# A GpSimd copy puts the first transposing load of x behind the first gate rows, one core, geglu FFN

## The chip, the cores and the metric

One core of a Trainium2 chip runs the whole kernel in one launch. The metric is the device time of that launch in microseconds (us); the time before is 273.48 us, the median of three runs (273.24, 273.48, 274.23). A difference of less than about 0.5% (1.37 us) can't be told from no change here.

## The reference

```python
B, S, D, F = 32, 32, 1024, 3584           # all inputs bf16
def reference(x, w_gate, w_up, w_down):
    return (_gelu(x @ w_gate) * (x @ w_up)) @ w_down   # tanh gelu
```

x is flattened to 1024 tokens by 1024 features. Random normal inputs, scaled by 0.05.

## The kernel before, in words

Both products are done by a Strassen-like scheme with seven half-size products (names with 11, 12, 21, 22 are the quadrants). Everything is written in an order of its own by hand (`tc.manual_schedule()`), so each engine's instructions stand in the order of the program text, and semaphores are put in where a tile is written and then read or written again. Semaphores of loads are taken in turn from eight slots, so a load also waits for the one eight loads before it.

Tokens are the columns (halves of `NB` = 512), features the rows (`DT` = 8 blocks of 128). `b11`, `b12`, `b21`, `b22` are the four quadrants of x with features on partitions; the first index is the feature half. `b21` is features 512 to 1023 of tokens 0 to 511: four blocks k = 0..3. Blocks 0 and 1 come by an ordinary load into `x_nat` and are transposed on TensorE in `transposed(dt)` (through `tp`, copied by VectorE into `b21`). Blocks 2 and 3 come by one transposing transfer, `load_xT(0, KD + KQ, DT)`. In the profile all four quadrants are named `b`.

The first work of TensorE is a set of products "ahead": gate columns in groups of `KB` = 4 blocks of 128, feature half 2 only, against `b21`. Group i has its weights in `a12_ahead[i]` (profile: `a12a` for i = 0, 1, `a12b` for i = 2 to 5), loaded by `load_ahead(i, k0, k1)`, where k0 to k1 are the feature blocks. `product_ahead(ps, i, j, k0, k1)` makes the matmuls; in the profile they are L288. The order on TensorE at the start is:

- `NWARM` = 6 matmuls on constants, to fill the time until `x_nat` lands (L258),
- `transposed(0)` (L266), then `NFILL` = 4 short 128-column matmuls on constants (L273),
- group 0, block k = 0, tokens 0 to 255 (four columns j), then `transposed(1)`, then the rest of k = 0 and 1 of group 0, in halves of 256 tokens,
- group 1, k = 0 and 1: eight matmuls of 512 columns,
- then, for each of the four columns of group 0, k = 2 and k = 3 in turn; then the same for group 1; then groups 2, 3, 4 and 5 with chunk 0's first product in between.

From there chunk follows chunk (`for ci in range(NCH)`, two column blocks of 128 each, seven products by `prod`, L277), with sums s1 to s4 of weights on GpSimd (L171 to L174) and t1 to t4 of x on VectorE (`tt`, L349 to L360). A second part multiplies by w_down (L429).

Loads stand on SyncE's queue (SP, L212 for `load_ahead`, L219 for transposing ones, L136 for the weight chunks) but for the probe, the second half of `x_nat` and k = 0, 1 of group 1, which are issued by ScalarE. SyncE's order around the change is: `x_nat` block 0; group 0 k = 0; group 0 k = 1; the transposing transfer of `b21` blocks 2, 3; group 0 k = 2, 3; group 1 k = 2, 3; groups 2 and 3 by halves; `wu` and `wg` of chunk 0; group 4; then `b11` and `b12` by transposing transfers, group 5, `b22`. GpSimd, after it has made `ident`, has nothing to do until `wu` has landed.

Of the kernel before, what the change touches and what calls it, by code (L numbers as in the profile page):

```python
# [13 lines left out]
def kernel(  # L14
# [20 lines left out]
    nc = tc.nc  # L35
# [14 lines left out]
    KD = DT // 2  # L50
# [4 lines left out]
    KQ = DT // 4  # L55
    HF = FT // 2
    MT = NB // P
    NWARM = 6
    NFILL = 4
    KB = 4  # L60
    QF = HF // 2
    batches = [(0, KB), (KB, QF), (QF, QF + KB), (QF + KB, HF)]
# [50 lines left out]
    a12_ahead = [ring.tile([P, KD, KB * P], bf16, name="a12a", tag="ring") for _ in range(2)]  # L113
    b11 = xpool.tile([P, KD, NB], bf16, name="b11")
    b21 = xpool.tile([P, KD, NB], bf16, name="b21")
# [81 lines left out]
    with tc.manual_schedule():  # L197
        def load_nat(eng, dt, p0, p1):
            eng.dma_start(  # L199
                out=x_nat[:, p0:p1, dt * P : (dt + 1) * P],  # L200
                in_=xf[p0 * P : p1 * P, (KD + dt) * P : (KD + dt + 1) * P].rearrange("(b p) d -> p b d", p=P),
            )
# [7 lines left out]
        def load_ahead(i, k0, k1, eng=nc.sync, j0=0, j1=KB):  # L210
            f0 = i * KB
            eng.dma_start(  # L212
                out=a12_ahead[i][:, k0:k1, j0 * P : j1 * P],
                in_=wg_r[:, KD + k0 : KD + k1, (f0 + j0) * P : (f0 + j1) * P],
            )

        def load_xT(nb, d0, d1):
            t = ((b11, b12), (b21, b22))[d0 // KD][nb]
            nc.sync.dma_start_transpose(  # L219
                out=t[:, d0 % KD : (d1 - 1) % KD + 1, :], in_=xf[nb * NB : (nb + 1) * NB, d0 * P : d1 * P]  # L220
            )

        load_ahead(0, 0, 1)
        load_nat(nc.scalar, 1, 0, NB_P)
        load_ahead(0, 1, 2)
        load_xT(0, KD + KQ, DT)
        load_ahead(1, 0, KQ, nc.scalar)
        a12_ahead += [spool.tile([P, KD, KB * P], bf16, name="a12b", tag=t) for t in ("s2", "s4", "s1", "s3")]
        for i in (0, 1):
            load_ahead(i, KQ, KD)  # L230
        def load_halves(i):
            for k in range(0, KD, KQ):
                load_ahead(i, k, k + KQ)
# [28 lines left out]
        def transposed(dt):  # L262
            for half, tp in enumerate(tps[dt]):
                p0 = half * HALF
                for b in range(HALF):
                    nc.tensor.transpose(  # L266
                        tp[:, b * P : (b + 1) * P], x_nat[:, p0 + b, dt * P : (dt + 1) * P], ident
                    )
                nc.vector.tensor_copy(b21[:, dt, p0 * P : (p0 + HALF) * P], tp)

        transposed(0)
        for _ in range(NFILL):
            nc.tensor.matmul(warm_ps[:, :P], lhsT=ones_w, rhs=ones_w, start=True, stop=True)  # L273
# [351 lines left out]
```

## Time and profile before

| | |
|---|---|
| median of three runs | 273.48 us |
| the profiled execution | 273.29 us |
| its span (first to last instruction) | 271.5 us |
| PE (TensorE) busy | 267.4 us (98%) |
| DVE (VectorE) / ACT (ScalarE) / POOL (GpSimd) busy | 202.8 / 115.6 / 120.2 us |
| moved by DMA | 35.86 MB, mean 132 GB/s |
| DMA share, 0 to 12 us | 7 to 9 tenths and more, in slices of 6.8 us |

Times inside the span are counted from its start; some 1.8 us of the execution lie around the span. A timeline row gives the start, how long the row lasted, the engine, the line and operation, out<-in, and how many instructions were merged; the bracket tells how long the engine sat idle before it and what ended that. A row of DMA issues gives out<-in, the issuing queue, the count, the size of one, and the median us from issue to landing. A queue's "DMA" row (SPq) is only the issue; the landing is later.

### The profile page before, as it was taken

How to read it: one execution, taken by the hardware profiler on the slowest of the kernel's cores; microseconds unless marked ns; L12 is line 12 of the kernel's file. 1: busy time of each engine (PE TensorE's matmuls, PEld its weight loads, DVE VectorE, ACT ScalarE, POOL GpSimd, SP SyncE). 2: the span in 40 equal slices, each digit the busy share in tenths (PEclk: the TensorE clock that was granted, in tenths of full speed). 3: DMA queues.
4: the chain of work that ended last, by engine and by line, in shares of the span. 5: the costliest groups of instructions: out<-in, count | busy, mean ns of one | idle time of the engine just before them, and what ended most of it. 6: DMA issues, size and time to landing. Idle time of an engine off the chain costs nothing.

```text
span 271.5 us, 3422 instructions
## 1 busy us (share of the span) xinstructions
PE 267.4 (98%) x1216; PEld 192.9 (71%) x1216; DVE 202.8 (75%) x205; ACT 115.6 (43%) x189; POOL 120.2 (44%) x60
## 2 busy tenths in 40 slices
PE   8999999999999999999999999999999999999995
PEld 4444776886787788688688687764458888888883
DVE  1448998886876876876776478469999999998621
ACT  2435766445544643745636635434000307870000
POOL 1090099977995994994994996000000000000000
DMA  7999230514505505505224290006981537865211
GB/s 173 325 245 251 52 104 21 150 38 117 157 1 153 156 2 155 139 15 157 81 76 127 49 325 4 0 2 202 356 253 60 158 112 260 273 196 163 73 42 58
DMA packets 56672, 35.86 MB, mean 132 GB/s; under 512 B 9936, under 2 KB 56656, under 8 KB 56656
## 3 DMA queue, kind: packets, MB, share of 16 engines
q1 hardware_dynamic: 53264, 33.17, 43.2%
q10 hardware_dynamic: 3392, 2.49, 2.8%
q8 instruction: 9, 0.15, 0.2%
q14 instruction: 7, 0.06, 0.1%
HBM read 31.72 MB, written 2.10 MB: 125 GB/s over the span
## 4 chain that ended last, share of the span: by engine, by line
PE 97%; DMA 1%; SPq 0%; DVE 0%; issue 0%
PE psA L277 38%; PE psA L429 24%; PE psC L277 19%; PE psC L429 7%; PE psA L288 5%; PE psC L288 3%; DMA a12a<-in_w_gate_dram 1%; PE psC L593 1%; SPq L199 0%; DVE o_last L594 0%; PE tp L266 0%
## 5 line engine op out<-in xcount | busy, mean ns | idle before, releaser
L277 PE MATMUL psA<-t,s 128*128 128x512 f32 x224 | 57.2, 397 | 0.0
L250 ACT ACTIVATE h<-c 128x512 bf16<-128x512 f32 x56 | 34.6, 629 | 41.6 <-DVE c L307 41.6
L277 PEld LDWEIGHTS psA<-t,s 128*128 128x128 f32 x224 | 42.1, 188 | 9.5
L171 POOL TENSOR_TENSOR s<-wu 128x1024 fp32r<-128x1024 bf16 x13 | 29.5, 2270 | 30.6 <-DMA wu<-in_w_up_dram 19.7
L172 POOL TENSOR_TENSOR s<-s,wg 128x1024 fp32r<-128x1024 f32 x14 | 32.0, 2284 | 15.0 <-DVE s L171 13.9
L277 PE MATMUL psA<-b,wg 128*128 128x512 bf16 x128 | 29.4, 380 | 0.0
L174 POOL TENSOR_TENSOR s<-wg,wu 128x1024 fp32r<-128x1024 bf16 x13 | 28.4, 2182 | 0.0
L277 PE MATMUL psA<-t,a22r 128*128 128x512 f32 x112 | 27.9, 391 | 0.0
L277 PE MATMUL psC<-t,s 128*128 128x512 f32 x112 | 27.9, 391 | 0.0
L277 PE MATMUL psC<-b22r,s 128*128 128x512 f32 x112 | 27.7, 389 | 0.0
L307 DVE TENSOR_TENSOR c<-sn,psA 128x512 f32<-128x512 f32 x32 | 21.8, 683 | 6.7 <-PE psA L277 5.9
L312 ACT COPY sn<-psC 128x512 f32<-128x512 f32 x28 | 16.3, 588 | 21.9 <-PE psC L277 14.9
L277 PEld LDWEIGHTS psC<-t,s 128*128 128x128 f32 x112 | 21.0, 188 | 4.5
L277 PEld LDWEIGHTS psA<-t,a22r 128*128 128x128 f32 x112 | 21.0, 188 | 4.5
L277 PEld LDWEIGHTS psC<-b22r,s 128*128 128x128 f32 x112 | 21.0, 188 | 4.4
L307 DVE TENSOR_TENSOR c<-sn,psC 128x512 f32<-128x512 f32 x28 | 19.2, 688 | 6.4 <-PE psC L277 6.4
L277 PEld LDWEIGHTS <-wg 128*128 128x128 bf16 x128 | 11.8, 98 | 15.3 <-issue 2.4
L406 DVE TENSOR_TENSOR lo<-c,h 128x512 bf16<-128x512 f32 x14 | 21.3, 1522 | 0.9
L173 POOL TENSOR_TENSOR s<-wg,s 128x1024 fp32r<-128x1024 bf16 x10 | 21.6, 2159 | 0.8
L312 ACT COPY sn<-psA 128x512 f32<-128x512 f32 x32 | 18.3, 592 | 5.5 <-PE psA L277 5.4
L307 DVE TENSOR_TENSOR c<-ahead,psA 128x512 f32<-128x512 f32 x24 | 16.4, 688 | 4.0 <-PE psA L277 2.4
L325 DVE TENSOR_TENSOR hi<-h,psA 128x512 bf16<-128x512 bf16 x14 | 9.6, 687 | 11.5 <-PE psA L277 11.5
(87 smaller groups left out, 381.1 us busy)
## 6 DMA issues: line engine op xcount, KB each, us to landing
wu<-in_w_up_dram SPq DMA_DIRECT2D x14, 512.0 KB, 4.0
wdb<-in_w_down_dram SPq DMA_DIRECT2D x12, 512.0 KB, 4.4
wg<-in_w_gate_dram SPq DMA_DIRECT2D x9, 512.0 KB, 5.1
wdb<-in_w_down_dram SPq DMA_DIRECT2D x12, 384.0 KB, 4.4
v<-in_w_down_dram SPq DMA_DIRECT2D x4, 512.0 KB, 6.2
out_dram<-o_sb ACTq DMA_DIRECT2D x15, 128.0 KB, 1.7
a12b<-in_w_gate_dram SPq DMA_DIRECT2D x6, 256.0 KB, 4.8
wg<-in_w_gate_dram SPq DMA_DIRECT2D x6, 256.0 KB, 4.7
```

The costliest lines, as they stand in the source:

```text
L171: yield engs[0].tensor_tensor(s1, a21, a22, ADD)
L172: yield engs[1].tensor_tensor(s2, s1, a11, SUB)
L173: yield engs[2].tensor_tensor(s4, a12, s2, SUB)
L174: yield engs[3].tensor_tensor(s3, a11, a21, SUB)
L250: nc.scalar.activation(h, src, ACT.Gelu_apprx_tanh)
L277: nc.tensor.matmul(ps, lhsT=lhs[:, k, :], rhs=rhs[:, k, :], start=(start and k == 0), stop=(k == KD - 1), skip_group_check=True,)
L288: nc.tensor.matmul(ps[:, cols], lhsT=a12_ahead[i][:, k, j * P : (j + 1) * P], rhs=b21[:, k, cols], start=(k == 0 and not cols.start), stop ...
L307: tt(t, s, ps, ADD)
L312: nc.scalar.copy(t, ps)
L325: tt(g_of(ft)[:, :NB], h0, psa, MUL)
L406: tt(g_of(ft)[:, NB:], added(sn5[fl], psa[fl]), h1[fl], MUL)
L429: nc.tensor.matmul(banks[m], lhsT=lhs(k)[:, m * P : (m + 1) * P], rhs=rhs(k), start=(start and k == 0), stop=(k == HF - 1), skip_group_che ...
```

## The change

Four things are edited. Group 0's k = 2 is loaded by a transfer of its own, which stands ahead of the transposing transfer, and k = 3 follows behind it. GpSimd copies one element of group 0's k = 0 into `b21`, where the transposing transfer will write; so the copy waits for that load, and the transposing transfer waits for the copy. The loads of group 1 (k = 2, 3) keep their order. Three short matmuls on constants are made in place of four.

```diff
-    NFILL = 4
+    NFILL = 3
...
         load_ahead(0, 0, 1)
         load_nat(nc.scalar, 1, 0, NB_P)
         load_ahead(0, 1, 2)
+        load_ahead(0, KQ, KQ + 1)
+        nc.gpsimd.tensor_copy(b21[:1, KQ, :1], a12_ahead[0][:1, 0, :1])
         load_xT(0, KD + KQ, DT)
         load_ahead(1, 0, KQ, nc.scalar)
         a12_ahead += [spool.tile([P, KD, KB * P], bf16, name="a12b", tag=t) for t in ("s2", "s4", "s1", "s3")]
-        for i in (0, 1):
-            load_ahead(i, KQ, KD)
+        load_ahead(0, KQ + 1, KD)
+        load_ahead(1, KQ, KD)
```

`KQ` is 2, `KD` is 4, `DT` is 8. SyncE has one instruction more, GpSimd one, TensorE one matmul and one weight load less; otherwise the order on every engine is as before.

## The prediction

> **What bounds the kernel now.** I read the chain that ended last first, by engine on the page, then its pieces of the first 14 us.
>
> ```profile
> PE 97%; DMA 1%; SPq 0%; DVE 0%; issue 0%
> ```
>
> ```profile
> 1.24 3.41 DMA a12a<-in_w_gate_dram
> 4.65 0.05 issue
> 4.70 0.39 PE psC L288 x2
> ```
>
> TensorE is the bound, and the only DMA on its chain is the load of group 0's k = 0 (issued at 1.24, landed at 4.65). TensorE's timeline shows the hole that it leaves and where the transferred blocks are first used:
>
> ```profile
> 3.71 0.49 PE L273 MATMUL psA<-const-bfloat16-1.0 128*128 128x128 bf16 x4
> 4.70 0.39 PE L288 MATMUL psC<-b,a12a 128*128 128x256 bf16 x2 [0.50 <-DMA a12a<-in_w_gate_dram]
> ...
> 8.44 1.03 PE L288 MATMUL psC<-b,a12a 128*128 128x512 bf16 x4
> 9.30 2.75 PE L288 MATMUL psA<-b,a12a 128*128 128x512 bf16 x12
> ```
>
> 0.50 us of idle end at 4.70; after that no row has a gap. The row at 8.44 is group 0 with k = 2 and 3: k = 2 and block 2 of `b21` are needed at 8.44, and k = 3 one matmul later, (9.30 - 8.44) / 4 = 0.22 on, at 8.66. Now SyncE's queue, and the landings of the issues at 2.25, 3.63, 15.66 and 19.68 (the DMA view of short windows around each):
>
> ```profile
> 1.24 0.96 SPq L212 DMA_DIRECT2D a12a<-in_w_gate_dram  x2
> 2.25 1.34 SPq L219 DMA_TRANSPOSE b<-in_x_dram  x1
> 3.63 1.08 SPq L212 DMA_DIRECT2D a12a<-in_w_gate_dram  x2
> 4.76 2.01 SPq L212 DMA_DIRECT2D a12b<-in_w_gate_dram  x4
> ```
>
> ```profile
> b<-in_x_dram SPq DMA_TRANSPOSE x1, 4.9
> a12a<-in_w_gate_dram SPq DMA_DIRECT2D x1, 256.0 KB, 4.3
> b<-in_x_dram SPq DMA_TRANSPOSE x1, 5.0
> b<-in_x_dram SPq DMA_TRANSPOSE x1, 5.3
> ```
>
> The transposing transfer lands at 2.25 + 4.9 = 7.15, so it has 1.3 us in hand; k = 2, 3 land at 3.63 + 4.3 = 7.93 and have 0.5 us. Those two small reserves are what the change spends.
>
> **The change part by part.**
>
> *The wait.* The transposing transfer can go out only when k = 0 has landed, GpSimd has copied, and SyncE has seen it. GpSimd's start after a landing: `wu`, issued at 6.81, landed 6.8 us later at 13.6, and its sum began at 13.74: 0.14. The copy itself isn't in the trace; the smallest GpSimd rows are 0.10 us (memsets of 128x1) and 0.29 (the select of `ident`). I take 0.15, as it is nearest to the smallest, and 0.06 for SyncE to go on (the gap between its issues is 0.05). That is 0.35 us after the landing, bounds 0.25 to 0.5: at 4.65 + 0.35 = 5.0 in place of 2.25. On GpSimd only the sum of 13.74 is queued behind the copy, so that costs nothing there. On SyncE every later load is queued behind it.
>
> *The transposing transfer itself.* Its price isn't one number: 4.9 us for this one of two blocks, 5.0 and 5.3 for the later ones of four blocks. The latter have 256 KB more, 0.9 us at the some 290 GB/s at which the DMA view of 16 to 17 us moves them, so 4.1 and 4.4 for two blocks. Bounds 4.1 to 4.9; I take 4.4, the row at 19.68, since it had only two loads in front of it, as here (k = 1 and k = 2 are the last ones before). It lands at 5.0 + 4.4 = 9.4.
>
> *k = 3.* It is issued when SyncE is through with the transposing issue (1.34 us), and goes through the same queue. Before, 256 KB landed 7.93 - 7.15 = 0.78 after the transposing transfer; 128 KB makes 0.39. So k = 3 lands at 9.4 + 0.39 = 9.8. It was needed at 8.66: TensorE ends its wait 1.1 us later than that matmul ran before. Block 2 alone (9.4 against 8.44) would cost 0.96; k = 3 comes last and decides. With the bounds of the price the shift is 0.8 to 1.6.
>
> *k = 2 ahead.* Issued at about 2.25 in the place of the transposing transfer, 128 KB, landed about as fast as its neighbour k = 1 (3.7 us, so near 6.0): long before 8.44. It takes nothing off the path, because its partner k = 3 is late. Without this edit k = 2 and 3 would land 0.39 later still.
>
> *What the freed start gives.* If k = 0 lands sooner, the 0.50 us of idle before 4.70 shrinks. But a TensorE that starts sooner only waits longer at k = 3; an earlier landing counts by letting the copy and the transfer go sooner. Does it land sooner? In the DMA view of 2.25 to 4.2 us the engines move some 200 GB/s, less than the 350 after 6.5 us, so there is something in the way. But the transposing packets are 256 B like those of `x_nat`, and the transfer was issued at 2.25, 1.01 us after k = 0. I take the landing unchanged, with 4.1 as the other bound (x_nat's 2.4 us after issue would give 3.64; TensorE has `b21` only by 4.0, when the first copy of the 0.51 us row at 3.74 is over).
>
> The Trainium skill, "DMA: Bandwidth & Descriptors", section "Rules for kernel authors", says that a transpose next to ordinary DMAs needs nothing, and that a DMA should be issued early and waited for late; by that the wait only spends reserve. No row here separates the two, since every transposing issue has others about it.
>
> *The fill.* One matmul of 128 columns less: (0.49 - 0.21) / 3 is about 0.1 us at most, hidden in the 0.50 of idle. If that cover is gone (k = 0 at 4.1) it is worth under 0.1 us, which the wait at k = 3 takes again.
>
> *What is queued behind on SyncE.* Group 1's k = 2, 3 had been issued at about 4.25; now SyncE reaches it at 5.0 + 1.34 + 0.55 + 0.1 = 7.0, 2.75 later. Landings move less, because the queue was full of data before: the transposing transfer is 9.4 - 7.15 = 2.25 later, less the 0.39 of k = 2 that went ahead, so about 1.9. Group 1's second half then lands at 8.7 + 1.9 = 10.6, needed at 10.16 + 1.1 = 11.3; group 2 at 9.4 + 1.9 = 11.3, needed at 11.89 + 1.1 = 13.0. The narrowest place behind is on VectorE:
>
> ```profile
> 20.80 2.29 DVE L349 TENSOR_TENSOR t<-b,b 128x2048 fp32r<-128x2048 bf16 x1 [1.10 <-DMA b<-in_x_dram]
> 25.13 2.29 DVE L355 TENSOR_TENSOR t<-b,t 128x2048 fp32r<-128x2048 bf16 x1 [0.26 <-DMA b<-in_x_dram]
> ...
> 39.10 0.68 DVE L307 TENSOR_TENSOR c<-sn,psA 128x512 f32<-128x512 f32 x1
> ```
>
> t1 and t2 wait for `b12` and `b22`, the last loads of this queue, and VectorE then works without a break until 41.7. Its add at 39.10 ends at 39.78 and must be over before TensorE goes on in that bank, in the second half of its row at 40.13 (L277, psA<-t,a22r, eight matmuls in 1.81), at 41.03: 1.25 us in hand. VectorE slides by 1.9, TensorE by 1.1: the reserve falls to 0.45 and holds.
>
> **The sum.** 273.29 + 1.1 = 274.4 against the profiled execution's own time (span 272.6). The median of the runs is 0.19 above it, which would make 274.6; I give 274.5.
>
> **The rivals.**
>
> *The first rows come sooner.* The transposing issue is what holds them up, and k = 0 lands at 4.1. For it: the low rate from 2.3 to 4. Against: its packets stand behind those of k = 0. The copy chain gives 4.45, the transfer 8.85, k = 3 9.25: 0.6 late, 273.29 + 0.6 = 273.9. (Bounds 0.3 to 1.1.)
>
> *A transposing transfer on a quiet queue is as quick as a plain one.* `x_nat` took 2.4 us for 128 KB; 0.4 more for the other half makes 2.8. It lands at 7.8, and k = 3, issued at 6.4, at 6.4 + 2.4 = 8.8, 0.14 late: 273.4. With the first rows at 4.1 as well, nothing is late, the 0.50 of idle is gone and the time is 272.8. Against: no transposing row is under 4.1 when brought to two blocks, and the issue alone takes 1.34. The Trainium skill, "DMA: Bandwidth & Descriptors", section "Anatomy of one DMA — SWDGE (gpsimd) path", has a fixed 2.0 us and 436 GB/s, for another issuing path; an estimate by it is 2.6 us for 256 KB, against the row's 4.9, so the trace disagrees.
>
> *Slower: the queue slides whole.* The later loads slide by SyncE's 2.75 us and not by 1.9. Then t1, t2 and the add of 39.10 slide by 2.75, over the 1.25 in hand, and TensorE is 1.5 late whatever it lost at k = 3: 274.8, 275.0 from the median, 0.55% up. It decides from a slide of 1.25 + 1.1 = 2.35 on. For it: the queue is served in order. Against: DMA is full from 6 us on, and a full queue slides by the hole in its data.
>
> *The clock falls in the wait.* The 128x512 matmuls of L258 show a mean of 623 ns against 379 later: TensorE starts at half rate. If a wait of over 1 us sent it back, up to 1.7 us more, 276. Against: the 0.50 us hole at 4.2 left the matmuls after it at full rate.
>
> **How the numbers follow.** The forecast (first rows unchanged, 0.8 to 1.6 late) 52%; first rows sooner 18%; transfer as quick as a plain one 7%, and with a gain 3%; the queue slides whole 14%; the clock 3%; 3% for a gain of over 0.5% that no row shows (all idle before 8.44 would have to go). Slower by over 0.5% (1.37 us; less can't be told from no change): the upper third of the forecast, 16%, with 14% and 3%: 33%. Faster 3%, the rest, 64%, within. The range leaves out the gains below and the clock above: 273.2 to 275.6; the forecast's own is 274.1 to 275.1.
>
> **What would show it.** Transposing issue on SyncE at about 5.0 and a GpSimd copy just before; L288 idle before k = 2 or 3, at 8.4 to 8.7, for about 1.1 us, released by a12a (or by `b`); none at 20 to 42. Wrong if that idle is absent or over 1.7, if the first L288 row starts before 4.4, or if TensorE has a gap behind VectorE near 41.

## The result, and the profile after

The changed kernel takes 274.83 us (median of 17 runs, 273.93 to 275.83), the kernel before 273.68 beside it (17 runs): ratio 1.0041, 95% interval 1.0027 to 1.0054, so 1.15 us slower, 0.7 to 1.5. With 17 runs of each this can be told from no change, though it lies under the 1.37 us named at the top. The profiled execution took 275.7 us, its span is 273.9, 2.4 more than before; 1.5 of that lies behind VectorE's last instruction, where only the last store is left (4.06 us in place of 2.54). Of the other profiles below one alone has such a tail (3.8 us, the kernel with the longer wait); a second profile of the changed kernel has 2.57. So the tail isn't counted to the change.

The chain by engine on the page, which was PE 97% and DMA 1% before:

```profile
PE 95%; issue 2%; DVE 2%; DVEq 0%
```

A load is no longer on it; VectorE is. SyncE's waits up to 10 us (who waited for whom: total, times, longest), GpSimd's timeline from 1 to 6 us and SyncE's timeline show the wait that was put in:

```profile
SPq L219 <- POOL b L227: 1.5, 1, 1.5
```

```profile
4.02 0.18 POOL L227 COPY b<-a12a 1x1 bf16<-1x1 bf16 x1 [2.71 <-DMA a12a<-in_w_gate_dram]
```

```profile
1.24 1.43 SPq L212 DMA_DIRECT2D a12a<-in_w_gate_dram  x3
4.22 1.34 SPq L219 DMA_TRANSPOSE b<-in_x_dram  x1
5.61 1.04 SPq L212 DMA_DIRECT2D a12a<-in_w_gate_dram  x2
6.70 2.00 SPq L212 DMA_DIRECT2D a12b<-in_w_gate_dram  x4
```

k = 0 landed at 3.96 (2.7 us after its issue, 3.4 before), the copy ran, and the transposing transfer went out at 4.22 in place of 2.25. What stands behind it on SyncE's queue goes out 1.9 to 2.0 us later (5.61 against 3.63, 6.70 against 4.76). The landings of the issues at 4.22 and at 5.61 (short windows of the DMA view):

```profile
b<-in_x_dram SPq DMA_TRANSPOSE x1, 3.3
a12a<-in_w_gate_dram SPq DMA_DIRECT2D x1, 128.0 KB, 3.1
```

The transposing transfer, 4.9 us before, takes 3.3, and is there at 7.53, only 0.4 later than before; k = 3 is there at 8.70. TensorE's timeline:

```profile
4.11 0.59 PE L290 MATMUL psC<-b,a12a 128*128 128x256 bf16 x2
5.77 0.61 PE L290 MATMUL psA<-b,a12a 128*128 128x256 bf16 x2
6.44 0.38 PE L290 MATMUL psA<-b,a12a 128*128 128x256 bf16 x2
8.82 1.03 PE L290 MATMUL psC<-b,a12a 128*128 128x512 bf16 x4
```

It starts on the gate rows at 4.11 in place of 4.70, but at half rate until 6.2 (0.6 us for two matmuls, then 0.38), and reaches k = 2 at 8.82, where k = 2, k = 3 and the transferred blocks are in: no gap there, 0.38 late. The gap is at 42 us. VectorE's timeline, TensorE's (before first, then after), and after's chain of work that ended last around it:

```profile
27.03 2.29 DVE L357 TENSOR_TENSOR t<-b,t 128x2048 fp32r<-128x2048 bf16 x1 [1.08 <-DMA b<-in_x_dram]
...
41.01 0.68 DVE L309 TENSOR_TENSOR c<-sn,psA 128x512 f32<-128x512 f32 x1
```

```profile
40.13 1.98 PE L277 MATMUL psA<-t,a22r 128*128 128x512 f32 x8
41.94 1.98 PE L277 MATMUL psC<-b22r,s 128*128 128x512 f32 x8
```

```profile
40.61 2.35 PE L279 MATMUL psA<-t,a22r 128*128 128x512 f32 x8
42.79 2.01 PE L279 MATMUL psC<-b22r,s 128*128 128x512 f32 x8
```

```profile
41.01 0.69 DVE c L309
...
41.74 1.21 PE psA L279 x4
```

t2 (VectorE's second sum of x) waits for `b22` until 27.03 (25.13 before), the add of 39.10 stands at 41.01, and TensorE goes on behind it at 41.74. TensorE was 0.48 late at 40.61 and is 0.85 late at 42.79. Its last product starts 0.88 later than before (before first, then after):

```profile
265.40 3.23 PE L593 MATMUL psC<-wdb,a_last 128*128 128x384 bf16 x28
```

```profile
266.28 3.23 PE L595 MATMUL psC<-wdb,a_last 128*128 128x384 bf16 x28
```

So between 43 and 266 us nothing more is lost.

### The profile page after: what moved, and what is told of

It is laid out like the page before. It is cut to its first block, busy times and chain, and to the rows that moved or that the text cites. A ratio compares the mean times of both kernels' runs of the same rounds, so it can differ in the third digit from the quotient of the medians.

```text
span 273.9 us, 3411 instructions
## 1 busy us (share of the span) xinstructions
PE 267.9 (98%) x1202; PEld 193.3 (71%) x1215; DVE 202.2 (74%) x205; ACT 115.6 (42%) x189; POOL 120.7 (44%) x61
## 4 chain that ended last, share of the span: by engine, by line
PE 95%; issue 2%; DVE 2%; DVEq 0%
PE psA L279 36%; PE psA L431 24%; PE psC L279 18%; PE psC L431 7%; PE psA L290 5%; PE psC L290 3%; DVE c L309 1%; PE psC L595 1%; PE psA L260 1%; PE tp L268 0%; DVE s L171 0%; PE psA L275 0%; DVE o_last L596 0%; DVE lo L408 0%; DVEq L309 0%
## 5 line engine op out<-in xcount | busy, mean ns | idle before, releaser
L174 POOL TENSOR_TENSOR s<-wg,wu 128x1024 fp32r<-128x1024 bf16 x13 | 29.4, 2261 | 0.0
L279 PE MATMUL psA<-b,wg 128*128 128x512 bf16 x119 | 27.8, 379 | 0.6
```

What stands on the lines that cost most here:

```text
L174: yield engs[3].tensor_tensor(s3, a11, a21, SUB)
L279: nc.tensor.matmul(ps, lhsT=lhs[:, k, :], rhs=rhs[:, k, :], start=(start and k == 0), stop=(k == KD - 1), skip_group_check=True,)
```

## The experiments

Three theories were set against each other. The queue theory: the wait makes SyncE's later loads late, `b22` last, and VectorE passes it on. The clock theory: TensorE's longer half rate at the start is the loss. The start theory: the wait lets the first gate rows land sooner. "After" below is the changed kernel; ratios are to the kernel before.

**The order without the wait.**

```diff
-        nc.gpsimd.tensor_copy(b21[:1, KQ, :1], a12_ahead[0][:1, 0, :1])
```

> The changed kernel without the copy: k = 2 goes ahead of the transposing transfer, three short matmuls, no wait. Queue theory (the time is lost because every load behind the wait comes about 1.9 us later, and VectorE's add near 41 us is late): the transposing issue is back near 2.7, b22 lands near 25, no gap near 42, 273.7 us as before (ratio 1.000, at most 0.001 off). Clock theory (TensorE's half rate lasts longer, to 6 us in place of 3.9, since a fill is missing): half rate to 6 us again, 0.4 to 1.1 us slower than before. Start theory (only the wait lets the first gate rows land early): k = 0 lands at 4.5 to 4.7 as before, not at 4.0.

273.55 us, ratio 0.9997 (0.9980 to 1.0015): no change. VectorE's timeline has t2 back:

```profile
24.86 2.29 DVE L356 TENSOR_TENSOR t<-b,t 128x2048 fp32r<-128x2048 bf16 x1 [0.15 <-DMA b<-in_x_dram]
```

So k = 2 as a transfer of its own and the missing fill cost nothing that can be told, though the half rate lasted to 4.9. k = 0 landed at 4.23, sooner than the 4.5 to 4.7 which the start theory asked for.

**The wait alone.**

```diff
         load_ahead(0, 1, 2)
+        nc.gpsimd.tensor_copy(b21[:1, KQ, :1], a12_ahead[0][:1, 0, :1])
         load_xT(0, KD + KQ, DT)
```

> The kernel before with the copy alone: k = 2 and 3 in one transfer behind the transposing one, four short matmuls. Queue theory: as slow as the changed kernel or up to 0.4 us slower, 274.6 to 275.2, with a gap near 42 us. Clock theory, if the fourth fill is what counts: full rate from 3.9 us, and 273.7 or less. Start theory: the first row of L288 starts near 4.1.

274.47 us, ratio 1.0034 (1.0015 to 1.0053): the loss belongs to the wait. It is 0.1 us under the expected 274.6; the gap near 42 is there, with 0.24 us. Here TensorE waits for k = 2 and 3 as well, where the prediction had put the loss; its timeline:

```profile
9.25 1.04 PE L289 MATMUL psC<-b,a12a 128*128 128x512 bf16 x4 [0.87 <-DMA a12a<-in_w_gate_dram]
```

The half rate lasted to 4.9 with four fills, as with three above.

**A longer wait.**

```diff
-        nc.gpsimd.tensor_copy(b21[:1, KQ, :1], a12_ahead[0][:1, 0, :1])
+        nc.gpsimd.tensor_copy(b21[:1, KQ, :1], a12_ahead[0][:1, 1, :1])
```

> The changed kernel with the copy reading k = 1 (landed at 5.16) in place of k = 0 (3.96): the wait is 1.2 us longer. Queue theory: b12 and b22 land 1.2 us later than in the changed kernel, VectorE's chain slides 1.2 more, the time is 1.2 us more, about 276.0, with a gap of about 1.5 us near 42 us or an equal one before it near 9 us. Clock theory: no change against the changed kernel, 274.8.

276.05 us (six runs), ratio 1.0084 (1.0064 to 1.0105): 1.2 us more than after, as the queue theory gives, and against the clock theory (full rate from 3.4 here, the soonest of all). SyncE's waits, and t2 on VectorE's timeline:

```profile
SPq L219 <- POOL b L227: 3.4, 1, 3.4
```

```profile
28.51 2.29 DVE L357 TENSOR_TENSOR t<-b,t 128x2048 fp32r<-128x2048 bf16 x1 [0.62 <-DMA b<-in_x_dram]
```

Up to 3 us this kernel does the same as after, and yet k = 0 landed at 5.04 and not at 3.96. So in this profile SyncE's wait is 1.9 us longer than in after's and not 1.2, and the last product 1.43 later: the way is as expected, and that the medians differ by just 1.2 is in part chance. TensorE waits in both places, 1.0 us for block 2 and k = 3 at 9 to 10 us and some 0.4 near 43.

**Less work on VectorE.**

```diff
-        chunk0 = sums(0, *[nc.gpsimd] * 3, nc.vector)
+        chunk0 = sums(0, *[nc.gpsimd] * 4)
```

> The changed kernel with chunk 0's sum s3 on GpSimd (idle from 20 to 34 us) and not on VectorE: VectorE's chain is 1.22 us shorter ahead of the add near 41 us. Queue theory: the gap near 42 us is gone, and only what TensorE is late at 8.8 us is left: 0.4 to 0.5 us less than the changed kernel, 274.3. Clock theory: the gap at 42 isn't what counts, so 274.8 as the changed kernel.

274.72 us, ratio 1.0042 (1.0020 to 1.0064): no better than after, so not what the queue theory expected. The timelines of GpSimd and VectorE say why this was no clean test:

```profile
22.61 2.12 POOL L174 TENSOR_TENSOR s<-wg,wu 128x1024 fp32r<-128x1024 bf16 x1
```

```profile
22.99 3.88 DVE L351 TENSOR_TENSOR t<-b,b 128x2048 fp32r<-128x2048 bf16 x1 [2.87 <-DMA b<-in_x_dram]
28.00 2.28 DVE L357 TENSOR_TENSOR t<-b,t 128x2048 fp32r<-128x2048 bf16 x1
```

GpSimd's sum came to lie beside t1 (VectorE's first sum of x), which took 3.88 us in place of 2.29; the 1.22 us taken off VectorE came back as 1.59, and TensorE waited 0.53 us for t2 itself.

**The adds first.** The same question without moving work:

```diff
                 prod(psa[fl], s3[fl], t3, False)
-                tt(g_of(ft)[:, NB:], added(sn5[fl], psa[fl]), h1[fl], MUL)
+                sn5[fl] = added(sn5[fl], psa[fl])
+            for fl, ft in enumerate(fts):
+                tt(g_of(ft)[:, NB:], sn5[fl], h1[fl], MUL)
```

> The changed kernel, with VectorE's two adds that read TensorE's bank (c<-sn,psA) made one after the other and the two long multiplications behind them, in every chunk: the add that TensorE waits for near 42 us comes 2 us earlier, GpSimd's work stays as it is. Queue theory, with VectorE as the last step: the gap near 42 us is gone, and of the 0.88 us that the changed kernel's last product is late only the lateness at 12 us is left (0.0 to 0.8, by how late k = 3 is): 274.2 to 274.6, 0.3 to 0.5 us less than the changed kernel. If k = 3 alone sets the end: no change against the changed kernel, 274.8.

274.36 us, ratio 1.0032 (1.0014 to 1.0051). On VectorE's timeline the second add is now 1.0 us behind the first and not 2.7, and TensorE's has no gap near 42:

```profile
37.98 0.69 DVE L309 TENSOR_TENSOR c<-sn,psA 128x512 f32<-128x512 f32 x1
39.02 0.69 DVE L309 TENSOR_TENSOR c<-sn,psA 128x512 f32<-128x512 f32 x1 [0.35 <-ACT h L252]
```

```profile
40.39 1.98 PE L279 MATMUL psA<-t,a22r 128*128 128x512 f32 x8
42.21 1.98 PE L279 MATMUL psC<-b22r,s 128*128 128x512 f32 x8
```

The last product is 0.26 late; 0.23 of it is there at 12.12 already (11.89 before), behind a wait for k = 3. In time that is 0.5 us less than after by the medians and 0.2 by the ratios, and the intervals overlap; that the add is the last step is shown by the profile, not by the time.

**The control: the same adds in the kernel before.**

> The kernel before with the same two adds first: the control. The add there has 1.25 us in hand, so both theories expect no change: 273.7, ratio 1.000, at most 0.001 off.

273.32 us, ratio 0.9991 (0.9977 to 1.0004): no change that can be told. Set beside this, the wait still costs 1.04 us (0.4%) with the adds first, nearly the 1.15 that it costs without, while the two profiles differ by 0.50 (265.66 and 265.16 in the table below). So the add isn't the only place with little in hand, and no run shows in time that moving it wins anything back; what is late in the executions that were not profiled is open.

**The transposing transfer later in the queue, with the wait.**

```diff
-        load_xT(0, KD + KQ, DT)
         load_ahead(1, 0, KQ, nc.scalar)
...
         load_ahead(0, KQ + 1, KD)
         load_ahead(1, KQ, KD)
+        load_xT(0, KD + KQ, DT)
```

> The changed kernel with the transposing transfer, its wait included, behind k = 3 and group 1's second half on SyncE's queue: the wait of SyncE falls to some 0.3 us, because it gets there at 3.9 when k = 0 has about landed. Queue theory (it is the idle SyncE that costs): b22 lands at 25 to 25.6, no gap near 42, block 2 of b21 lands near 8.2: 273.4 to 273.9, the time of before. If it is the later transposing issue that costs and not what stands behind it: 274.6 to 274.8.

273.94 us, ratio 1.0017 (1.0001 to 1.0033): less than half of the loss by the middle values, though the interval overlaps with that of after. SyncE's timeline and VectorE's:

```profile
1.24 2.38 SPq L212 DMA_DIRECT2D a12a<-in_w_gate_dram  x5
4.67 1.34 SPq L219 DMA_TRANSPOSE b<-in_x_dram  x1
```

```profile
26.35 2.29 DVE L357 TENSOR_TENSOR t<-b,t 128x2048 fp32r<-128x2048 bf16 x1 [0.99 <-DMA b<-in_x_dram]
```

Two loads have moved out of the idle time. It was still 1.0 us long, not 0.3, since k = 0 landed at 4.41; `b22` came later than expected for the same reason, and the last product is 0.15 late. The transposing issue itself is later than in after (4.67 against 4.22) and the time is less: by the middle values, what stands behind it counts.

**The late place without the wait.**

> The same late place of the transposing transfer, without the copy, so without a wait. Queue theory: 273.4 to 273.9, equal to the one with the wait within 0.2 us. Start theory (the wait lets the first gate rows land early): L288 starts at 4.2 to 4.7 here and at 4.1 with the wait; if landings of k = 0 scatter by themselves, there is no such order.

273.63 us, ratio 1.0002 (0.9985 to 1.0020): as before. The transposing issue is at 3.67 and SyncE is never idle. The first row on gate rows starts at 4.28, sooner than the 4.46 with the wait, against the start theory.

**The order without the wait, with the adds first.**

> What the experiments point to: no wait, k = 2 on its own ahead of the transposing transfer, the two adds first. Queue theory: b22 lands near 24.7, TensorE without a gap from 4.3 on, 273.2 to 273.5, at most 0.2% under the kernel before and 1.2 us under the changed kernel. A theory in which the adds alone make up for the wait gives no more than the 0.4 us that they gave there.

273.67 us, ratio 1.0007 (0.9985 to 1.0028): not a version that beats the kernel before. TensorE waits for no load behind 4.52 us in it, but the half rate lasted to 5.7, and the last product is 0.41 late by that alone.

**The changed kernel, a second profile.**

> The changed kernel once more, for a second profile of it. Queue theory: gap near 42 us again, TensorE's last product (L595) 0.8 to 1.3 us later than the 265.40 of before, whenever the clock goes up. Clock theory: if the clock goes up near 4 to 5 us, as in four of the other profiles, the last product is at most 0.5 us late.

276.07 us in its one run, above the slowest of after's 17. TensorE was at full rate by 4.66, where its gate rows start, and the last product 2.57 late: against the clock theory, and twice what the queue theory had expected. k = 0 landed at 4.62 and SyncE stood until 4.88; `b22` came 3.6 us late. Now several reserves are used up, in TensorE's timeline and VectorE's:

```profile
25.32 1.90 PE L290 MATMUL psC<-b,a12b 128*128 128x512 bf16 x8 [0.62 <-DMA a12b<-in_w_gate_dram]
...
31.20 2.09 PE L279 MATMUL psA<-t,s 128*128 128x512 f32 x8 [0.41 <-DVE t L357]
```

```profile
28.77 2.29 DVE L357 TENSOR_TENSOR t<-b,t 128x2048 fp32r<-128x2048 bf16 x1 [1.50 <-DMA b<-in_x_dram]
...
42.75 0.67 DVE L309 TENSOR_TENSOR c<-sn,psA 128x512 f32<-128x512 f32 x1
```

**All profiles together.** The start of t2 on VectorE beside the start of TensorE's last product. t2 waits for `b22`, but in three profiles VectorE was busy until it started: late without the wait, order with the adds first, and the one with less work on VectorE.

| kernel | t2 starts | last product starts | between |
|---|---|---|---|
| before | 25.13 | 265.40 | 240.27 |
| order without the wait | 24.86 | 265.26 | 240.40 |
| late, without the wait | 24.85 | 265.32 | 240.47 |
| late, with the wait | 26.35 | 265.55 | 239.20 |
| after | 27.03 | 266.28 | 239.25 |
| the wait alone | 27.23 | 266.44 | 239.21 |
| wait for k = 1 | 28.51 | 267.71 | 239.20 |
| after, second profile | 28.77 | 267.97 | 239.20 |
| before, adds first | 24.82 | 265.16 | 240.34 |
| order, adds first | 25.18 | 265.81 | 240.63 |
| after, adds first | 26.68 | 265.66 | 238.98 |
| after, less on VectorE | 28.00 | 266.64 | 238.64 |

In all five profiles with the wait and VectorE's work unchanged, the last product follows t2 at 239.20 to 239.25 us, whatever TensorE did up to then. In the profiles without the wait there is 1.07 us or more in hand. With the wait and VectorE's work changed (the last two rows) the 239.2 is undercut: it was VectorE's chain from t2 to the add.

## Why the prediction came out

The forecast was 1.1 us on the profiled execution; by the medians it is 1.15. The number held, and the place was another: the one that the third rival named, not k = 3. All three signs that the prediction gave for being wrong are in the profile of after: no idle time at 8.4 to 8.7, gate rows from 4.11 on, and a gap behind VectorE at 42. So it was luck that the 1.1 us forecast for one wait fits a loss that came about at another. The third rival's time, 274.8 to 275.0, takes in the measured 274.83, but by a slide of 2.75 us, where 1.9 was measured.

- **The wait** was priced at 0.35 us after the landing of k = 0, with 0.25 to 0.5 as bounds: 0.26 (3.96 to 4.22), of it 0.18 for the copy (0.15 taken).
- **The first rows** were forecast to land as before. They landed 0.69 sooner in the profile of after, as the first rival had it. That the wait brings this isn't shown: k = 0 landed at 4.62 in after's second profile and at 5.04 with the longer wait, but at 3.91 to 4.10 in the other profiles with the wait in its first place, and at 4.11 to 4.65 in the five kernels without one.
- **The transposing transfer** is the term that was mis-sized: 4.4 taken, 4.1 to 4.9 as bounds, 3.3 measured, 3.0 to 3.3 in the six profiles in which SyncE stood until k = 0 (or k = 1) had landed, with at most k = 1 and 2 ahead. All rows it was taken from had other loads about them; the five kernels without the wait show 4.4 to 4.9 again. The second rival (2.8) was nearer.
- **k = 3** was to land at 9.8, and TensorE to idle 1.1 us near 8.7. It landed at 8.70, and no gap showed, since the half rate had made TensorE as late. The other profiles with the wait in its first place do show the forecast wait, shorter: 0.17 to 0.70 us for k = 3, and 0.87 where k = 2 and 3 are one load. That step of the sum failed with the term before it, and where VectorE's work was unchanged the end was set by t2 all the same.
- **The slide of the later loads**, 1.9, was measured: 27.03 - 25.13. But it was derived from a transposing transfer 2.25 us late, which was 0.4 late. SyncE's later issues slid by 1.9 to 2.0, which is the rival's mechanism: the idle time of the queue goes through to its end. The landings took it up by degrees: 0.8 us for group 1's second half (forecast 1.9), 1.7 for `b12`, 1.9 for `b22`. Over the profiles with the wait in its first place it ran from 1.6 to 3.6.
- **VectorE's reserve** was put at 1.25 us and said to hold, because TensorE itself would be 1.1 late. It is 1.07 by the table (240.27 less 239.20), TensorE was only 0.48 late, and so it decided in the profile of after: 1.90 less 1.07 is 0.83, and 0.85 was measured at 42.79. The third rival's point (from 2.35 on) had the same failed 1.1 in it.
- **The fill** costs nothing, and **the clock** did not fall in a wait: behind the longest, 1.16 us up to 5.09 with the longer wait, two matmuls of 256 columns took 0.39 as at full rate. That the half rate at the start could last longer was on no list; it cost the 0.41 of the order with the adds first and hid the wait for k = 3 in after.

The scatter of the runs of after is not settled: the second profile differs from the first in the landing of k = 0 (0.66) and in `b22` (1.73), and what made the loads in between still later was not tried. Why k = 0 lands anywhere from 3.9 to 5.0 stays open too. It isn't late alone: ScalarE's half of `x_nat` landed at 4.30 to 4.81 in the seven profiles with k = 0 by 4.24, and at 4.89 to 5.45 in the five with k = 0 at 4.41 or later.

## What to carry to other kernels

A wait put into a queue that issues loads holds up all that stands behind it, and the price is read at the queue's last consumer, not at the transfer that waits: here, in the profile, 1.9 us of slide met 1.07 us in hand on VectorE, 18 to 37 us later. For each load behind the wait, write down what it has in hand before trusting that a bound engine will hide it. If one transfer must go later, let the others pass it first, which took back more than half of this loss by the middle values (the intervals overlap).

## What the runs showed of the hardware

- The transposing transfer of 256 KB took 4.4 to 4.9 us when issued at 2.2 to 3.7 us into a filling queue, 3.8 at 4.67 behind four loads of SyncE still under way, and 3.0 to 3.3 at 4.2 to 6.1 behind k = 1 and 2 at most. The 3.3 was with the DMA engines moving 315 GB/s (4.23 to 5.5), a 3.0 with 4 GB/s (6.1 to 7.4, the longer wait).
- TensorE's half rate ended anywhere from 3.4 to 6.2 us in twelve profiles whose first 3.3 us are the same on TensorE: 4.9 with three fills and 4.9 with four. The Trainium skill, "TensorE: Matmul & The Clock Gate", section "Part 1: The HAM clock gate (the "warmup" mystery)", says that the clock is judged in a free-running window of some 3.4 us, so that the point of change varies from run to run. The spread of 2.8 us is within such a window, but far over the 500 ns either way that the section gives for it; the measurement decides.
- In the one place where a GpSimd sum of 128x1024 (22.61 to 24.73) lay beside VectorE's t1 of 128x2048, t1 took 3.88 us in place of 2.29.
